# Attention with decaying state and a two-expert adapter: loads in tile order, two-chunk frames, unread products at the start, shared copies and a new order

## The chip, the core and the metric

The kernel runs on one core of one Trainium2 chip. A core has five engines that run their own instruction streams and meet at semaphores: TensorE (PE, with its weight loads shown apart as PEld), VectorE (DVE), ScalarE (ACT), GpSimd (POOL) and SyncE (SP), which issues most transfers. Sixteen DMA engines move data between HBM and the on-chip memory SBUF; PE writes its products to PSUM, which has eight banks. The metric is device time in microseconds (us): 98.98 is the median of three runs (98.64 to 99.32).

## What is computed

Four sequences with eight heads, 768 tokens and 48 channels pass a linear attention whose state decays by w per token and channel; the outputs of the heads, side by side (384 channels), get the weighted sum of the two best of eight rank-16 adapters:

```python
for t in range(S):                                   # per batch and head
    cur = einsum('bhd,bhe->bhde', u[None] * kt, vt)
    y[:, :, t] = einsum('bhd,bhde->bhe', rt, state + cur)
    state = wt[..., None] * state + einsum('bhd,bhe->bhde', kt, vt)
...
logits = x @ w_gate                                  # x: y as (3072, 384)
topk = the 2 largest of 8; w = softmax over these 2
out = x + sum over the 2 experts e of w[e] * (x @ A[e]) @ B[e]
```

## The kernel before

The work is cut into 24 tiles of 128 tokens: four sequences of six tiles. Heads are handled in four pairs; a pair stands on 128 partitions as two heads of 48 channels, each padded to 64 with zeros. One tile passes these steps (functions of the same names; lines as in the profile):

- **Loads.** load_rk brings r and k of a tile (512 KB) into a ring of ten (RING), load_w brings w of two tiles (384 KB; tiles 0 and 1 alone), both issued by SP. load_v is issued by POOL and turns v into bf16 on the way: one, two and three chunks at the start, then six at a time, into four buffers. consts.0, consts.1 and consts.2 load u, the matrix A with the gate, and B; castc (L164, POOL) turns them into bf16.
- **Decay.** ln (L176, ACT) takes log w; cs (L186, PE) sums it along the tile with four products with a triangle of ones, into x_ps, a single bank; expp (L191, ACT) and expm (L196, ACT) make the exponentials of plus and minus that sum.
- **Products with the decay.** rmul (L205, POOL) makes rd from r and expp, kmul (L210, DVE) makes kd_ from k and expm, qmul (L200, POOL) makes q = r k.
- **The own token.** dgmm (L228, PE) multiplies q with u per pair, four products of eight columns; dv (L241, DVE) scales v with the result; ymd (L280, PE) adds it to y_ps.
- **Inside the tile.** amm (L249, PE) multiplies kd_ with rd into a_ps, aev (L254, DVE) masks it into at, ymv (L295, PE) multiplies that with v into y_ps.
- **The state.** ktr (L223, PE) transposes kd_, ktev (L235, ACT) copies it to ks, kv (L264, PE) adds ks times v to the state s_ps, resc (L270, DVE) scales the state with the tile's whole decay, and sev (L275, ACT) copies it to sb; ymS (L289, PE) multiplies the previous tile's sb with rd into y_ps. The last tile of a sequence does none of the state's steps but ymS.
- **The output of attention.** yev (L300, ACT) copies y_ps to xT.
- **The gate**, for three tiles at once (the last three tiles as two and one): zl (L314, PE) makes logits and x A; top (L326 and L328, DVE) finds the largest and the differences, gexp (L334, ACT), gsel (L340, DVE), gmul (L347, POOL), gnorm (L353 and L354, DVE) and gmul2 (L360, POOL) make the weights g, zw (L366, DVE) scales x A, zT (L375, PE) transposes it, zTev (L381, DVE) copies it.
- **The result.** dmm (L389 and L391, PE) adds x and the adapters' share in PSUM, oev (L396, ACT) copies to res, store (L400, SP) writes it.

PSUM is full: a_ps takes two banks, x_ps, kd, y_ps and s_ps one each, and z_ps, zT_ps and d_ps share two.

The order of each engine's instructions is written out by hand in ORDER, a list of "step.tile"; an engine takes its own steps from it strictly in that order, and semaphores see to what it needs from others. A step whose engine waits holds everything behind it on that engine. The list was made by a planner from costs of the steps.

## Time and profile before

| | |
|---|---|
| median of three runs | 98.98 us |
| the profiled execution | 97.83 us, its span 96.1 us |
| busy: PE, DVE, ACT, POOL | 73.8, 75.6, 72.9, 67.0 us |
| mean granted clock of PE | 0.987 |
| DMA | 25.09 MB, mean 261 GB/s |

The span runs from the first to the last instruction of one profiled execution; the rest of its 97.83 us lies around it. A row of a group gives busy time, mean duration of one, and the idle time of its engine just before, with what ended it. Durations of neighbours on an engine overlap a little, so that sums of durations are longer than the busy time.

### The profile page before, as it was taken

To read this page: it belongs to the slowest core of one execution; us is meant where nothing else is said; L and a number is where in the kernel's file an instruction comes from. 1 tells how busy PE (TensorE), PEld (TensorE's weight loads), DVE (VectorE), ACT (ScalarE), POOL (GpSimd) and SP (SyncE) were. 2 spreads that over 40 slices of the span, in tenths; PEclk is the share of its full clock that TensorE was granted. 3 is DMA by queue.
4 is the path that set the end of the run, shared out by engine and by line. 5 is a ranking of instruction groups with operands and counts; after the bars stand their busy time and mean duration, and the time that the engine had idled before them with its cause. 6 is when DMAs were issued, how large, how long until landed. Compare 5 with 4: busy or idle time off the path is not lost.

```text
span 96.1 us, 3361 instructions
## 1 busy us (share of the span) xinstructions
PE 73.8 (77%) x1312; PEld 56.5 (59%) x1312; DVE 75.6 (79%) x180; ACT 72.9 (76%) x159; POOL 67.0 (70%) x85
## 2 busy tenths in 40 slices
PE   0204069999989997999899889989998898987230
PEld 0103057787867775787778667867776695754010
DVE  5423427978599999999999999999999999984320
ACT  5347148785699789999999989999999996663410
POOL 7581089996099969999999589899918997200000
PEclk9999999999999999999999999999999999999995
DMA  2999999999999506999999999889618842215402
GB/s 56 318 243 285 317 412 422 413 419 312 275 412 380 201 24 162 388 322 215 375 422 406 403 409 229 237 291 405 238 51 240 328 159 96 83 67 186 163 1 82
DMA packets 10096, 25.09 MB, mean 261 GB/s; under 512 B 1248, under 2 KB 4960, under 8 KB 10080
## 3 DMA queue, kind: packets, MB, share of 16 engines
q1 hardware_dynamic: 9216, 22.52, 62.5%
q0 software_dynamic: 864, 2.36, 13.3%
q8 instruction: 10, 0.16, 0.7%
q14 instruction: 6, 0.05, 0.2%
HBM read 22.51 MB, written 4.72 MB: 283 GB/s over the span
## 4 chain that ended last, share of the span: by engine, by line
DVE 39%; PE 36%; issue 11%; POOL 4%; ACT 4%; DMA 3%; POOLq 0%; ACTq 0%; DVEq 0%
DVE at L254 11%; DVE dv L241 6%; PE z_ps L314 5%; PE y_ps L295 5%; PE kd L223 4%; PE x_ps L186 4%; PE a_ps L249 4%; DVE zw L366 3%; DVE s_ps L270 3%; PE y_ps L280 3%; PE y_ps L289 3%; DMA w_in<-in_w_dram 3%; PE d_ps L391 2%; DVE tp L326 2%; PE kd L228 2%
## 5 line engine op out<-in xcount | busy, mean ns | idle before, releaser
L254 DVE TENSOR_TENSOR at<-a_ps,mask 128x1024 bf16<-128x1024 f32 x24 | 29.1, 1213 | 3.6 <-PE a_ps L249 3.6
L200 POOL TENSOR_TENSOR q<-rk 128x512 bf16<-128x512 f32 x24 | 30.2, 1267 | 0.0
L205 POOL TENSOR_TENSOR rd<-rk,ep 128x512 bf16<-128x512 f32 x24 | 28.1, 1179 | 1.8 <-ACT ep L191 1.6
L191 ACT ACTIVATE ep<-x_ps 128x512 f32<-128x512 f32 x24 | 14.4, 602 | 5.1 <-PE x_ps L186 4.7
L186 PE MATMUL x_ps<-tri,lw 128*128 128x128 f16 x96 | 10.7, 242 | 8.1 <-ACT lw L176 6.9
L300 ACT CAST xT<-y_ps 128x512 bf16<-128x512 f32 x24 | 14.1, 590 | 2.7 <-PE y_ps L295 2.7
L396 ACT COPY res<-d_ps 128x384 f32<-128x384 f32 x24 | 11.3, 490 | 4.6 <-PE d_ps L391 4.1
L196 ACT ACTIVATE x_ps<-x_ps 128x512 f32<-128x512 f32 x24 | 14.4, 601 | 0.0
L241 DVE TENSOR_TENSOR dv<-v_bf,kd 128x384 bf16<-128x384 bf16 x24 | 13.0, 544 | 1.2 <-PE kd L228 1.1
L186 PEld LDWEIGHTS <-lw 128*128 128x128 f16 x96 | 6.7, 107 | 10.4 <-ACT lw L176 7.5
L176 ACT ACTIVATE lw<-w_in 128x768 f16<-128x768 f32 (+1 forms) x13 | 10.3, 793 | 2.7 <-DMA w_in<-in_w_dram 2.7
L347 POOL TENSOR_TENSOR pe<-sel,ge 128x24 f32<-128x24 f32 (+2 forms) x9 | 2.1, 228 | 13.9 <-ACT ge L334 9.5
L295 PE MATMUL y_ps<-at,v_bf 128*48 128x128 bf16 x192 | 10.4, 233 | 1.3 <-DVE at L254 1.1
L235 ACT COPY ks<-kd 128x384 bf16<-128x384 bf16 x20 | 9.6, 482 | 2.0 <-PE kd L223 1.5
L280 PE MATMUL y_ps<-ident,dv 128*128 128x128 bf16 x96 | 10.0, 231 | 0.1
L289 PE MATMUL y_ps<-rd,sb 48*48 48x128 bf16 x160 | 8.5, 229 | 0.7 <-ACT sb L275 0.7
L228 PE MATMUL kd<-ub,q 128*128 128x8 bf16 x96 | 6.1, 169 | 3.9 <-POOL ub L164 3.9
L295 PEld LDWEIGHTS <-v_bf 128*48 128x48 bf16 x192 | 6.7, 107 | 3.4 <-issue 1.6
L391 PE MATMUL d_ps<-b_b,zT 128*128 128x384 bf16 x24 | 7.8, 327 | 0.4 <-DVE zT L381 0.2
L389 PE MATMUL d_ps<-ident,xT 128*128 128x96 bf16 x96 | 8.1, 207 | 0.0
L314 PE MATMUL z_ps<-aw_b,xT 128*128 128x136 bf16 x96 | 7.8, 235 | 0.3 <-ACT res L396 0.3
L270 DVE TENSOR_TENSOR s_ps<-s_ps,ep 128x192 f32<-128x192 f32 x20 | 7.2, 359 | 0.9 <-PE s_ps L264 0.7
(151 smaller groups left out, 130.1 us busy)
## 6 DMA issues: line engine op xcount, KB each, us to landing
rk<-in_rk_dram SPq DMA_DIRECT2D x24, 512.0 KB, 8.2
out_dram<-res SPq DMA_DIRECT2D x24, 192.0 KB, 2.9
w_in<-in_w_dram SPq DMA_DIRECT2D x11, 384.0 KB, 8.3
v_bf<-in_v_dram POOLq DMA_DIRECT2D x3, 576.0 KB, 9.0
w_in<-in_w_dram SPq DMA_DIRECT2D x2, 192.0 KB, 3.9
v_bf<-in_v_dram POOLq DMA_DIRECT2D x1, 288.0 KB, 8.8
aw_f<-in_aw_dram SPq DMA_DIRECT2D x1, 272.0 KB, 10.2
v_bf<-in_v_dram POOLq DMA_DIRECT2D x1, 192.0 KB, 7.6
```

The lines of the kernel that those rows point to most:

```text
L186: nc.tensor.matmul(x_ps[:, p, :], lhsT=lwof(t, p), rhs=tri, start=True, stop=True)
L191: nc.scalar.activation(out=ep[:, :, 1:L + 1], in_=st[t]["x"], func=ACT.Exp)
L196: nc.scalar.activation(out=x, in_=x, func=ACT.Exp, scale=-1.0)
L200: nc.gpsimd.tensor_mul(q, st[t]["rk"][:, 0], st[t]["rk"][:, 1])
L205: nc.gpsimd.tensor_mul(rd, st[t]["rk"][:, 0], st[t]["ep"][:, :, 0:L])
L241: nc.vector.tensor_mul(o[:, :, 0:D], vseq[t], dg.to_broadcast([128, H, D]))
L254: nc.vector.tensor_mul(at.rearrange("s g p f -> s (g p) f"), st[t]["a_ps"].rearrange("s g p f -> s (g p) f"), mask.to_broadcast([128, H, L]))
L280: nc.tensor.matmul(y_ps[:, p, :], lhsT=st[t]["dv"][:, 2 * p:2 * p + 2, :].rearrange("p a b -> p (a b)"), rhs=ident, start=(p == 0), stop=F ...
L289: nc.tensor.matmul(st[t]["y_ps"][s_, p, :], lhsT=st[t - 1]["sb"][s_, p, :], rhs=st[t]["rd"][s_, p, :], start=False, stop=False, skip_group ...
L295: nc.tensor.matmul(st[t]["y_ps"][g * 64:g * 64 + D, p, :], lhsT=vseq[t][:, h, :], rhs=st[t]["at"][:, g, p, :], start=False, stop=(h >= H - ...
L300: nc.scalar.copy(out=xT, in_=st[t]["y_ps"])
L314: nc.tensor.matmul(z_ps[:, i, :], lhsT=st[t0 + i]["xT"][:, p, :], rhs=aw_b[:, p, :], start=(p == 0), stop=(p == P - 1))
```

## The change

- Rings: twelve rk tiles instead of ten, four buffers of log w instead of three, q three instead of two, rd six instead of three, kd_ five instead of two, res six instead of four. v comes in loads of three chunks into six buffers.
- Loads are listed strictly by tile on SP. The first is followed by rk.0, w.1, u, rk.1, w.2 and so on up to rk.14 ahead of the first store; rk.15 to rk.21 follow store.5.
- warm(n) issues n products of 512 columns of zeros into a bank that nobody reads: nine ahead of cs.0, seven behind it, five behind cs.1 and two behind cs.2.
- Filled pads: the sixteen pad rows of the first three pairs carry pieces of the fourth pair's r and k, so qmul works on three pairs instead of four and dgmm issues three products instead of four. The values are only placed by the host.
- Two-chunk frames: the running sum of the decay goes over two tiles. An odd tile's cs has four more products (with ones, over the tile before); expp writes into a frame of two tiles (four of them); resc is done behind odd tiles only.
- Shared copies: some ktev, sev, oev move to DVE, some zTev to ACT, rmul.1 and castc.2 to DVE.
- For the last gate (one tile) gsel and gmul become one DVE instruction, and gmul2 and zw another.
- ORDER is a new list.

The diff, cut:

```diff
+PQ = P - 1
-RING = 10
+RING = 12
+VL = 3
+VB = 6
+Q_ON_DVE = ()
+R_ON_DVE = (1,)
+CAST_ON_DVE = (2,)
+KT_ON_DVE = (0, 1, 2, 6, 12)
+S_ON_DVE = (1, 6, 8, 16)
+Y_ON_DVE = ()
+OUT_ON_DVE = (10, 15, 22)
+ZT_ON_ACT = (2, 17, 20)
 ORDER = """
...
+warm.9 load_v.0 load_v.1 load_w.0 load_rk.0 ln.0 cs.0 warm.7 load_w.1 expp.0 ln.1 expm.0 rmul.0 kmul.0 amm.0
+aev.0 cs.1 warm.5 expp.1 expm.1 consts.0 castc.0 load_rk.1 qmul.1 rmul.1 load_w.2 load_rk.2 ln.2 load_rk.3
+load_w.4 load_rk.4 qmul.0 dgmm.0 load_v.3 kmul.1 amm.1 cs.2 warm.2 aev.1 expp.2 expm.2 rmul.2 dv.0 ktr.0
+ymd.0 ktev.0 ymv.0 kv.0 yev.0 sev.0 qmul.2 kmul.2 dgmm.1 dv.1 amm.2 aev.2 cs.3 expp.3 expm.3 rmul.3 ktr.1
+ktev.1 ymd.1 ymS.1 ymv.1 kmul.3 dgmm.2 dv.2 kv.1 resc.1 sev.1 ln.4 cs.4 ktr.2 ktev.2 yev.1 ymd.2 ymS.2
+qmul.3 dgmm.3 dv.3 expp.4 expm.4 kmul.4 kv.2 load_v.6 sev.2 amm.3 aev.3 ktr.3 ktev.3 ymv.2 yev.2 cs.5 expp.5
...
+aev.10 gexp.8 gmul.8 gnorm.8 gmul2.8 cs.12 expp.12 expm.12 rmul.12 dmm.5 oev.5 store.5 load_v.15 kv.10
+sev.10 dgmm.11 dv.11 qmul.14 qmul.13 kmul.12 ymd.10 ymS.10 ymv.10 yev.10 zw.8 amm.11 aev.11 dgmm.12 dv.12
+cs.13 expp.13 expm.13 rmul.13 zT.8 zTev.8 ln.14 ymd.11 ymS.11 ymv.11 yev.11 load_rk.15 qmul.15 load_w.16
+load_rk.16 load_rk.17 load_w.18 load_rk.18 load_rk.19 load_w.20 load_rk.20 load_rk.21 amm.12 ktr.12 dmm.7
+oev.7 store.7 kmul.13 cs.14 expp.14 expm.14 rmul.14 dmm.6 oev.6 store.6 ktev.12 dgmm.13 aev.12 dv.13 zl.11
...
+aev.23 dmm.18 oev.18 store.18 zl.22 kv.22 sev.22 top.22 gexp.22 gsel.22 gmul.22 gnorm.22 dmm.20 oev.20
+store.20 ymd.23 ymS.23 ymv.23 yev.23 gmul2.22 zw.22 zT.22 zTev.22 dmm.21 dmm.22 oev.21 oev.22 store.21
+store.22 zl.23 top.23 gexp.23 gmul.23 gnorm.23 zw.23 zT.23 zTev.23 dmm.23 oev.23 store.23
 """
+    zero = const.tile([128, 512], BF16)
+    nc.vector.memset(zero, 0.0)
+    ones = const.tile([128, 128], FP16)
+    nc.vector.memset(ones, 1.0)
-    NLW = 3
+    NLW = 4
-    NEP = 3
+    NEP = 4
-        t_ = const.tile([128, P, L + 1], F32, name=f"ep{i}")
+        t_ = const.tile([128, P, WL * L + 1], F32, name=f"ep{i}")
+    def warm(n):
+        if not idle:
+            idle["ps"] = pp.tile([128, 512], F32, name="idle_ps", tag="m", bufs=2)
+        for _ in range(n):
+            nc.tensor.matmul(idle["ps"], lhsT=zero[:, 0:128], rhs=zero, start=True, stop=True)
+    def copy(on_dve, o, i):
+        if on_dve:
+            nc.vector.tensor_copy(out=o, in_=i)
+        else:
+            nc.scalar.copy(out=o, in_=i)
-        n = {0: 1, 1: 2, 3: 3}[t] if t < NC else NC
-        v_bf = wk.tile([128, NC, H, D], BF16, name="v_bf", bufs=4)
+        n = {0: 1, 1: 2, 3: 3}[t] if t < NC else VL
+        v_bf = wk.tile([128, VL, H, D], BF16, name="v_bf", bufs=VB)
-            nc.tensor.matmul(x_ps[:, p, :], lhsT=lwof(t, p), rhs=tri, start=True, stop=True)
+            nc.tensor.matmul(x_ps[:, p, :], lhsT=lwof(t, p), rhs=tri, start=True, stop=t % WL == 0)
+            if t % WL:
+                nc.tensor.matmul(x_ps[:, p, :], lhsT=lwof(t - 1, p), rhs=ones, start=False, stop=True)
-        nc.gpsimd.tensor_mul(q, st[t]["rk"][:, 0], st[t]["rk"][:, 1])
+        (nc.vector if t in Q_ON_DVE else nc.gpsimd).tensor_mul(q, st[t]["rk"][:, 0, 0:PQ], st[t]["rk"][:, 1, 0:PQ])
-        for p in range(P):
+        for p in range(PQ):
...
-        if t % NC < NC - 1:
+        if t % WL == WL - 1 and t % NC < NC - 1:
             d_ = st[t]["ep"][:, :, L:L + 1]
             nc.vector.tensor_mul(s_ps, s_ps, d_.to_broadcast([128, P, D]))
...
+        if n == 1:
+            nc.vector.scalar_tensor_tensor(out=pe[:, 0], in0=st[t]["z_ps"][:, 0, ER:ER + E], scalar=st[t]["tp"][:, 0, 1:2],
+                                           in1=st[t]["ge"][:, 0], op0=ALU.is_ge, op1=ALU.mult)
...
+    for j in range(2 * PQ):
+        c = j % 3 * 16
+        rk[:, :, j % 2, D:64, :, j // 2] = rk[:, :, j // 3, c:c + 16, :, PQ]
```

## The prediction

> **What bounds the kernel now.** I read the page's slices first, then a table of busy time by stage, then the chain of waits, the groups of instructions and the DMA views.

> ```profile
> span 96.1 us, 3361 instructions
> PE   0204069999989997999899889989998898987230
> DVE  5423427978599999999999999999999999984320
> DMA  2999999999999506999999999889618842215402
> ```

> The slices are 2.4 us each. VectorE (DVE) is full from slice 12 to slice 35, and has holes ahead of that and behind it. The stages, cut at instructions that I name below (columns: busy time of PE, PEld, DVE, ACT, POOL with counts, granted clock, DMA share, GB/s):

> ```profile
> 7.55:12.57 5.02, 1.15 (x12) 0.79 (x13) 1.91 (x2) 1.84 (x3) 0.27 (x3) 1.00 1.11 312
> 12.57:16.40 3.83, 3.63 (x49) 2.76 (x49) 2.06 (x4) 2.82 (x6) 3.83 (x4) 1.00 1.03 416
> 16.40:20.40 4.00, 4.00 (x55) 3.36 (x56) 3.64 (x5) 3.07 (x7) 3.98 (x5) 1.00 1.03 416
> 20.40:24.40 4.00, 4.00 (x55) 3.17 (x53) 2.87 (x5) 2.90 (x7) 2.74 (x3) 1.00 1.06 341
> 29.08:79.66 50.58, 47.12 (x923) 36.78 (x919) 49.78 (x117) 48.34 (x109) 45.02 (x49) 1.00 0.81 277
> 84.28:96.10 11.82, 4.74 (x68) 3.03 (x66) 4.21 (x17) 3.66 (x10) 0.84 (x4) 0.89 0.27 101
> ```

> Three regimes. The middle (29.08 to 79.66, seventeen tiles, 2.98 us each) belongs to DVE: 49.78 of 50.58 us, with ACT (48.34) and PE (47.12) close behind. The start holds a hole (7.55 to 12.57, in which every compute engine is idle for more than half the time while the DMA engines are full) and then a stretch in which PE is full and DVE isn't. The end is a chain of single instructions. The start in detail, from the order of time, where a bracket gives the idle time before and its releaser, and from the chain (the lines with two numbers, a name and a count):

> ```profile
> 6.97 0.52 ACT L176 ACTIVATE lw<-w_in 128x384 f16<-128x384 f32 x1 [1.40 <-DMA w_in<-in_w_dram]
> 11.08 0.69 DVE L210 TENSOR_TENSOR kd__180<-rk,x_ps 128x512 bf16<-128x512 f32 x1 [1.04 <-DMA rk<-in_rk_dram]
> 12.31 0.21 POOL L164 CAST ub<-ub_f 128x32 bf16<-128x32 f32 x1 [4.75 <-DMA ub_f<-in_ublk_dram]
> 14.42 0.69 DVE L210 TENSOR_TENSOR kd__217<-rk,x_ps 128x512 bf16<-128x512 f32 x1 [1.01 <-ACT x_ps L196]
> 28.99 0.68 DVE L210 TENSOR_TENSOR kd__537<-rk,x_ps 128x512 bf16<-128x512 f32 x1
> 14.05 0.43 PE y_ps L280 x4
> 23.86 1.37 PE z_ps L314 x12
> 29.08 0.59 DVE kd__537 L210
> 39.77 0.22 PE y_ps L280 x4
> ```

> The hole is the wait for the small u load (POOL until 12.31) and for tile 1's rk (DVE until 11.08). The three kmul lines with brackets or shapes are tiles 1, 2 and 6; the chain has tile 6's again with 0.59, its time without the 0.09 in which it overlaps the instruction before. The two L280 lines are the same four products of 128 columns: 0.43 us early, 0.22 later, while the granted clock reads 1.00 in both stages. So PE ran at half its later rate from 12.57 until about the z products at 23.86, although it was busy for 11.63 of those 11.83 us.

> [...]

> **The change part by part: the start.** Durations, by groups (busy us, mean ns):

> ```profile
> L254 DVE TENSOR_TENSOR at<-a_ps,mask 128x1024 bf16<-128x1024 f32 x24 | 29.1, 1213 | 3.6 <-PE a_ps L249 3.6
> L241 DVE TENSOR_TENSOR dv<-v_bf,kd 128x384 bf16<-128x384 bf16 x24 | 13.0, 544 | 1.2 <-PE kd L228 1.1
> L270 DVE TENSOR_TENSOR s_ps<-s_ps,ep 128x192 f32<-128x192 f32 x20 | 7.2, 359 | 0.9 <-PE s_ps L264 0.7
> L381 DVE COPY zT<-zT_ps 128x384 bf16<-128x384 bf16 x7 | 2.4, 349 | 0.0
> L326 DVE MAX8 tp<-z_ps 128x8 f32<-128x8 f32 x24 | 2.6, 161 | 2.9 <-PE z_ps L314 2.5
> L366 DVE TENSOR_TENSOR zw<-z_ps,g 128x384 bf16<-128x384 f32 x7 | 3.9, 550 | 0.1
> L164 POOL CAST b_b<-b_f 128x384 bf16<-128x384 f32 x1 | 0.5, 499 | 0.0
> L200 POOL TENSOR_TENSOR q<-rk 128x512 bf16<-128x512 f32 x24 | 30.2, 1267 | 0.0
> L235 ACT COPY ks<-kd 128x384 bf16<-128x384 bf16 x20 | 9.6, 482 | 2.0 <-PE kd L223 1.5 <-ACT xT L300 0.2
> L396 ACT COPY res<-d_ps 128x384 f32<-128x384 f32 x24 | 11.3, 490 | 4.6 <-PE d_ps L391 4.1
> L191 ACT ACTIVATE ep<-x_ps 128x512 f32<-128x512 f32 x24 | 14.4, 602 | 5.1 <-PE x_ps L186 4.7
> rk<-in_rk_dram SPq DMA_DIRECT2D x24, 512.0 KB, 8.2
> v_bf<-in_v_dram POOLq DMA_DIRECT2D x1, 288.0 KB, 8.8
> q0 software_dynamic: 432, 0.59, 31.5%
> ```

> The last line is the v queue in the first 12 us: 31.5% of 12 us, 3.8 us of all DMA engines, for six chunks of v. The change leaves three of them for later (1.9 us freed), and puts w.2 (384 KB) behind rk.1 and u ahead of both. At 312 GB/s w.2 is 1.2 us. So rk.1 should land some 3 us earlier than 11.08, near 8, and u earlier than that. The hole shrinks, and what bounds the start instead is a chain that the warm-up makes longer: nine unread products of 512 columns at 0.43 us, from about 1.2 us, hold PE until 5.0, so cs.0 ends at 5.6. ACT now takes ln.1 ahead of expm.0, and w.1 lands at 6.97: ln.1 ends at 7.5, expm.0 (taken as L191) at 8.1, kmul.0 (0.69) at 8.8, amm.0 (two times 0.3) at 9.4, aev.0 (1.21) at 10.6. Then, all on DVE: rmul.1 (moved from POOL; priced as kmul, 0.69, the other end L200's 1.27) to 11.3, kmul.1 to 12.0, 0.6 for amm.1, aev.1 to 13.8, dv.0 (0.54) to 14.4, ktev.0 to 14.7. kmul.2 starts at 14.7, against 14.42 before, but with aev.1, rmul.1 and ktev.0 done. The small cast moves only within POOL, and qmul.1 ahead of qmul.0 is covered by rmul.1's and amm.1's times.

> From kmul.2 to kmul.6 the new order gives DVE three more kmul besides kmul.2 (0.59 each), four dv (0.46), three aev (1.14), resc.1 and resc.3 and sev.1 (0.28 each), two ktev (0.30), the gate of tiles 0 to 2 (three tp, four small ones taken as tp, zw: 7 x 0.16 + 0.55, and less the overlap 1.6) and the cast of B (0.45, by its 0.50 on POOL). Each is its group's mean less some 0.08 of overlap. That is 2.36 + 1.84 + 3.42 + 0.84 + 0.60 + 1.6 + 0.45 = 11.1 us. kmul.6 would start at 25.8 if DVE never waited. One wait shows: load_v.3 is behind qmul.0 on POOL, so it is issued near 11.3 and lands at 20.1 (8.8), and dv.3 is due at 19.3. I put 0.6 us down for it and its like: kmul.6 at 26.4 instead of 28.99, **-2.6 us**; without any wait -3.2. This needs PE at full rate. Nothing before 12.57 is as dense as the warm-up, and the flip came at the z products, the first long run of wide full-height products; so I take it as warm. The cover gone (PE cold until 24 us), the gain is about 0: the stretch is PE's as before, with three odd tiles' extra products (3 x 0.43 = 1.3) against its start 1.1 us earlier.

> **The middle.** From kmul.6 on, resc falls from sixteen to six; tile 22's lies beside the gate's chain and counts nothing: 9 x 0.359 = -3.2. Shared copies: ktev 6 and 12 on DVE by the zT copy of the same size, 2 x 0.349 (ACT's 482 ns the other end) = +0.7; sev 6, 8, 16 by L270, 3 x 0.359 = +1.1; oev 10, 15, 22 by dv, 3 x 0.544 (ACT's 490 the other end) = +1.6; zTev 2, 17, 20 away, -1.05. Sum **-0.8**. ACT loses two 482, three 490 and three sev and gets two zT back, POOL loses a quarter of q (24 x 0.32 = 7.6 by size; 0 if q has a fixed price). Neither sets the pace, so neither counts. POOL pays three more v issues. The wider rings for q, rd, kd_, res and lw, the two-frame ep and the memsets (before the first load lands) cost nothing on the path.

> PE pays: each odd tile issues four more products of 128 columns, 0.22 to 0.38 us, nine tiles, +2.0 to +3.4; the fourth product of dgmm goes (the filled pads carry it), 17 x 0.05 = -0.8.

> ```profile
> 38.65 0.38 PE x_ps L186 x4
> 38.27 0.19 PE kd L228 x4
> rk<-in_rk_dram SPq DMA_DIRECT2D x1, 512.0 KB, 4.2
> ```

> Net +1.2 to +2.6 against the 3.46 us in which PE idles in the middle. The new order's waits can't be read off a profile of the old one. Ends: -0.8 (DVE's 0.80 idle goes) and +2.6 (PE sets the pace and keeps its idle time). I take **+0.8**, nearer to the cover than to its loss, since DVE waited only 0.80 us under the old order.

> **The end.** The last gate, one tile:

> ```profile
> 90.50 0.20 POOL L347 TENSOR_TENSOR pe<-sel,ge 128x8 f32<-128x8 f32 x1 [3.32 <-ACT ge L334]
> 90.93 0.16 DVE L354 RECIPROCAL den<-den 128x1 f32<-128x1 f32 x1
> 91.24 0.20 POOL L360 TENSOR_TENSOR g<-pe,den 128x8 f32<-128x8 f32 x1 [0.54 <-DVE den L354]
> 91.47 0.29 DVE L366 TENSOR_TENSOR zw<-z_ps,g 128x128 bf16<-128x128 f32 x1 [0.38 <-POOL g L360]
> ```

> gmul2's step goes: zw follows den at once, 91.12 instead of 91.47. gmul on DVE saves about 0.05. oev.22 on DVE stands beside oev.21, and zl.23 still waits for oev.21. **-0.4.**

> **Sum.** -2.6 - 0.8 + 0.8 - 0.4 = -3.0. The profiled execution took 97.83 us (span 96.1), so 94.8 by its own; it lies 1.15 below the median of the runs, 98.98, to which I apply the sum: 96.0.

> **The rivals.**

> PE stays cold (B). For it: 11.63 busy of 11.83 us did not warm it before. Against: the warm-up is denser. The start gains nothing: 98.98 - 0.8 + 0.8 - 0.4 = 98.6. The unread products would then be without effect on the rate.

> PE becomes the pace of the middle (C): +2.6 instead of +0.8, 97.8. For it: 47.12 of 50.58 busy already. Against: busy counts pipelined ends, and 3.46 us are free.

> Late loads of tiles 15 to 21 (D), the slower side. On SP they now stand behind store.5, which waits for oev.5, behind expm.12. From the end T of expp.12, oev.5 ends at T + 1.1 (0.60 + 0.49), and rk.15 lands at T + 1.1 + L. POOL reaches qmul.15 behind rmul.13, which follows expp.13 (T + 3.0, one tile on), so by T + 4.3 (1.27, as L200), and rmul.14, due at T + 6, stands behind qmul.15 (0.95): late by L + 1.1 + 0.95 - 6 = L - 3.95. With L = 4.2, seen once in a quiet stretch, that is 0.3 and hidden; with the median 8.2 it is 4.25, and the time is 96.0 + 4.25 = 100.2. It turns slower than before by 1% at L = 7.9. Against it, by then the first fifteen tiles are in, and the queue is empty.

> **How the numbers follow.** About 1% is what a measurement of this kernel can tell from no change: 97.99 to 99.97. Forecast 0.57 (96.0; its own range 92.8 to 97.9: all terms at their good ends, -3.2 - 0.8 - 0.8 - 0.4 = -5.2, give 93.8, less one for the 1.15 between profile and median), C 0.11 (97.8, still faster), B 0.15 (98.6, same), D 0.17 (100.2, slower). Faster 0.68, same 0.15, slower 0.17. The range, 92.8 to 99.0, takes in B and leaves out D and a little at the low end.

> **What would show it.** Right: L280's groups take 0.22 before 15 us; POOL's wait for u ends before 9; kmul.6 starts near 26.4; DVE stays over 97% busy from there to aev.23; the last den to zw gap is under 0.05. Wrong: 0.43 at 20 us (B); PE at 98% with DVE waiting for PE in the middle (C); POOL waiting for a DMA near tile 15 (D); or dv waiting for v, which I priced for tile 3 alone.

## The result and the profile after

The changed kernel takes 94.99 us (median of six runs, 94.59 to 96.03), the kernel before 98.81 in the runs beside it: a ratio of 0.968, interval 0.960 to 0.977. The forecast was 96.0. Ratios here and below compare only those executions of each kernel that lie within some 1.5% of its fastest, medians take in all of them, so the two need not agree.

The profiled execution of the changed kernel happens to be the longest of its six (96.03 us, span 94.3), while that of the kernel before lies below its median. A second profile of the very same kernel, taken for the first experiment, has a span of 91.6. The two differ above all in the granted clock, so both are shown: the one below is "after", the other "again".

The page's slices of after:

```profile
span 94.3 us, 3426 instructions
DVE  5803965978999999999999999989999998974620
PEclk9999995559999999999999999999999999999955
```

And of again:

```profile
span 91.6 us, 3426 instructions
DVE  5907778989999999999999999999989998973710
PEclk9999999999999999999999999999999999999855
```

The granted clock of after is at half (0.50) in slices 7 to 9 (14.0 to 20.8 us); again keeps it until the last slices. The order of time in after, at the places that the prediction named:

```profile
7.78 0.20 POOL L197 CAST ub<-ub_f 128x24 bf16<-128x24 f32 x1 [0.24 <-DMA ub_f<-in_ublk_dram]
9.83 2.40 POOL L236 TENSOR_TENSOR q<-rk 128x384 bf16<-128x384 f32 x2 [1.84 <-DMA rk<-in_rk_dram]
15.01 0.63 PE L316 MATMUL y_ps<-ident,dv 128*128 128x128 bf16 x4
15.53 0.68 DVE L246 TENSOR_TENSOR kd__275<-rk,x_ps 128x512 bf16<-128x512 f32 x1
18.25 0.63 PE L316 MATMUL y_ps<-ident,dv 128*128 128x128 bf16 x4
28.46 0.67 DVE L246 TENSOR_TENSOR kd__614<-rk,x_ps 128x512 bf16<-128x512 f32 x1
89.26 0.16 DVE L397 RECIPROCAL den<-den 128x1 f32<-128x1 f32 x1
89.45 0.35 DVE L412 SCALAR_TENSOR_TENSOR zw<-z_ps,den,pe 128x128 bf16<-128x128 f32 x1
```

The wait for u is gone (12.31 before), tile 1's rk lands at 9.8, and ymd's four products (L316, L280 before) still take 0.63 us from first start to last end, as in this view of the kernel before at half rate (16.73 us; 0.38 at 27.53, at full rate). In again the same four, and tile 6's kmul:

```profile
13.82 0.39 PE L316 MATMUL y_ps<-ident,dv 128*128 128x128 bf16 x4
26.00 0.68 DVE L246 TENSOR_TENSOR kd__614<-rk,x_ps 128x512 bf16<-128x512 f32 x1
```

With PE at full rate tile 6's kmul starts at 26.00, without it at 28.46, against 28.99 before. The table of stages for the stretch from that kmul to the last aev (columns as in the prediction), before, after and again:

```profile
28.99:84.28 55.29, 51.47 (x1007) 39.90 (x1004) 54.03 (x126) 51.41 (x116) 47.04 (x52) 1.00 0.76 262
```

```profile
28.46:82.60 54.14, 52.21 (x1012) 41.27 (x1010) 52.96 (x121) 50.22 (x112) 43.39 (x53) 1.00 0.80 266
```

```profile
26.00:79.92 53.92, 52.26 (x1012) 41.20 (x1010) 52.92 (x122) 50.08 (x112) 43.26 (x53) 1.00 0.83 284
```

DVE works 1.1 us less and waits 1.2 and 1.0 us instead of 1.3; PE works 0.8 us more. Behind it, from the last aev's start to the span's end, lie 11.82 us before, 11.70 after and 11.68 in again. So against the profile before, start, middle and end change by -0.5, -1.2 and -0.1 us in after, and by -3.0, -1.4 and -0.1 in again.

### The profile page after: what moved, and what is told of

Same layout as the page of the kernel before. It is cut to its first block, busy times and chain, and to the rows that moved or that the text cites. A ratio compares the mean times of both kernels' runs of the same rounds, so it can differ in the third digit from the quotient of the medians.

```text
span 94.3 us, 3426 instructions
## 1 busy us (share of the span) xinstructions
PE 80.9 (86%) x1359; PEld 59.7 (63%) x1359; DVE 77.6 (82%) x183; ACT 69.9 (74%) x150; POOL 61.2 (65%) x84
## 3 DMA queue, kind: packets, MB, share of 16 engines
q0 software_dynamic: 1296, 2.36, 14.1%
## 4 chain that ended last, share of the span: by engine, by line
DMA 42%; DVE 23%; PE 9%; SPq 8%; issue 7%; ACT 4%; POOL 3%; POOLq 0%; ACTq 0%
DMA rk<-in_rk_dram 35%; DVE at L290 9%; DMA w_in<-in_w_dram 7%; SPq L180 4%; SPq L174 4%; DVE dv L277 3%; DVE zw L419 2%; ACT res L163 1%; PE d_ps L444 1%; PE z_ps L350 1%; DVE den L396 1%; POOL q L236 1%; POOL pe L390 1%; PE d_ps L442 1%; PE zT_ps L428 1%
## 5 line engine op out<-in xcount | busy, mean ns | idle before, releaser
L241 POOL TENSOR_TENSOR rd<-rk,ep 128x512 bf16<-128x512 f32 x23 | 27.2, 1183 | 9.1 <-ACT ep L227 9.0
L236 POOL TENSOR_TENSOR q<-rk 128x384 bf16<-128x384 f32 x24 | 24.3, 1020 | 2.4 <-DMA rk<-in_rk_dram 2.2
L163 ACT COPY res<-d_ps 128x384 f32<-128x384 f32 x21 | 10.2, 484 | 5.2 <-PE d_ps L444 4.5
L219 PE MATMUL x_ps<-tri,lw 128*128 128x128 f16 x96 | 12.1, 230 | 0.8 <-DVE kd__1701 L246 0.3
L316 PE MATMUL y_ps<-ident,dv 128*128 128x128 bf16 x96 | 9.8, 227 | 0.1
L219 PEld LDWEIGHTS <-lw 128*128 128x128 f16 x96 | 8.1, 102 | 2.6 <-issue 1.2
L157 PE MATMUL idle_ps<-zero 128*128 128x512 bf16 x23 | 8.4, 523 | 1.2 <-DVE zero L102 1.2
L163 ACT COPY ks<-kd 128x384 bf16<-128x384 bf16 x15 | 7.3, 487 | 0.9 <-PE kd L259 0.5
L350 PE MATMUL z_ps<-aw_b,xT 128*128 128x136 bf16 x96 | 7.2, 223 | 0.2 <-ACT res L163 0.2
L316 PEld LDWEIGHTS <-dv 128*128 128x128 bf16 x96 | 6.8, 102 | 0.5 <-issue 0.2
L221 PE MATMUL x_ps<-ones,lw 128*128 128x128 f16 x48 | 7.0, 227 | 0.0
## 6 DMA issues: line engine op xcount, KB each, us to landing
rk<-in_rk_dram SPq DMA_DIRECT2D x24, 512.0 KB, 10.2
v_bf<-in_v_dram POOLq DMA_DIRECT2D x7, 288.0 KB, 7.0
```

The costliest lines, as they stand in the source:

```text
L163: nc.scalar.copy(out=o, in_=i)
L219: nc.tensor.matmul(x_ps[:, p, :], lhsT=lwof(t, p), rhs=tri, start=True, stop=t % WL == 0)
L236: (nc.vector if t in Q_ON_DVE else nc.gpsimd).tensor_mul(q, st[t]["rk"][:, 0, 0:PQ], st[t]["rk"][:, 1, 0:PQ])
L241: (nc.vector if t in R_ON_DVE else nc.gpsimd).tensor_mul(rd, st[t]["rk"][:, 0], st[t]["ep"][:, :, 0:L])
L316: nc.tensor.matmul(y_ps[:, p, :], lhsT=st[t]["dv"][:, 2 * p:2 * p + 2, :].rearrange("p a b -> p (a b)"), rhs=ident, start=(p == 0), stop=F ...
```

## The experiments: what the start is made of

**Again, more unread products, none, and qmul.0 first.** Four kernels on one chip, 98.31 us for the kernel before there. The first is the changed kernel with no edit.

> The changed kernel once more, beside the others on one chip. Theory (call it rate): the profiled execution shows a granted clock of 0.50 from 14 to 20 us, and executions differ in how long that lasts (0.935 to 0.978 mean clock); so a second look should give 94.6 to 95.6 us, and a span that is shorter where the mean clock is higher. Rival (chain): the start is set by loads and by the order on POOL, the clock doesn't matter; then span and mean clock go without relation.

Measured: 95.17 us (93.35 to 95.90), ratio 0.976 (0.961 to 0.991). Over the twelve executions of both sets, the five with a mean clock of 0.935 to 0.938 have spans of 93.3 to 94.3 (mean 93.8), the seven with 0.961 to 0.978 have 91.6 to 93.7 (mean 92.8). So a lower clock goes with a span longer by about one us; it doesn't explain all of the scatter. The kernel before scatters more (95.86 to 101.45 over its 18 executions here).

```diff
-warm.9 load_v.0 load_v.1 load_w.0 load_rk.0 ln.0 cs.0 warm.7 load_w.1
+load_v.0 load_v.1 load_w.0 load_rk.0 ln.0 cs.0 load_w.1
...
-cs.1 warm.5
+cs.1
...
-cs.2 warm.2
+cs.2
```

> The changed kernel without the 23 unread products. Rate theory: PE stays at half rate until the z products, as before the change; the start loses what the warm-up gives, 1 to 2 us, so 96 to 97 us, and tile 6's kmul comes at 29 to 30 us. Chain rival: the unread products only delay cs.0 (5.0 instead of 3.8 us), so without them 94 to 95 us, no slower than the changed kernel.

Measured: 97.93 us, ratio 1.007 (0.999 to 1.015): by the ratio nothing of the change's gain is left. Tile 6's kmul comes at 28.12, and the profile has a second loss, which the rate has no part in. Its middle is 55.29 us long, as long as before the change, because of this (POOL, then DVE):

```profile
52.72 1.00 POOL L236 TENSOR_TENSOR q<-rk 128x384 bf16<-128x384 f32 x1 [2.07 <-DMA rk<-in_rk_dram]
55.08 0.18 DVE L396 TENSOR_REDUCE den<-pe 128x3 f32<-128x24 f32 x1 [1.52 <-POOL pe L390]
```

That is qmul.15: POOL waits for rk.15, which SP issued at 46.38, behind store.5; the gate's step behind it on POOL comes late, and DVE stands. It is the prediction's rival D, at a landing time of at most 6.3 us and a price of 1.2 (55.29 against 54.14).

```diff
-cs.0 warm.7
+cs.0 warm.9
...
-cs.1 warm.5
+cs.1 warm.11
...
-cs.2 warm.2
+cs.2 warm.7
```

> The changed kernel with 36 unread products instead of 23 (9, 9, 11 and 7), which fill PE's idle time ahead of amm.0, dgmm.0 and ktr.0. Rate theory: the granted clock no longer falls to 0.50, dv and ktev no longer wait for PE, tile 6's kmul comes near 27 us instead of 28.5, and the time falls by 1 to 1.5 us to about 93.7. Chain rival: no change within 0.5 us.

Measured: 94.69 us (93.91 to 94.92), ratio 0.985 (0.976 to 0.994). In its profile the granted clock stays at 1.00 through the start (4 to 28 us) and tile 6's kmul comes at 26.52, span 92.3. So the fall was kept off here, and all six executions lie within 1.0 us, where again's spread over 2.5. The median isn't lower by the 1 to 1.5 us expected: only some executions of the changed kernel have the fall, and where there is none, tile 6's kmul comes half a us later than in again (26.52 against 26.00).

```diff
-castc.0 load_rk.1 qmul.1
+castc.0 qmul.0 load_rk.1 qmul.1
...
-load_rk.4 qmul.0 dgmm.0
+load_rk.4 dgmm.0
```

> The changed kernel with qmul.0 ahead of qmul.1 on POOL, so that it no longer stands behind the wait for tile 1's rk (landed at 9.8 us); dgmm.0 could run near 10 instead of 12.3. Chain rival: the start moves up by up to 1.5 us, 93.5 us. Rate theory: amm.1 still waits for kmul.1 (12.0 us), so no more than 0.4 us, but the gap on PE is shorter, and with it the fall of the clock perhaps later.

Measured: 96.17 us, ratio 0.986 (0.968 to 1.005). dgmm.0 ran at 10.39 instead of 12.29, and amm.1 came no earlier (12.99, 12.45 in after). It waits for kmul.1, which stands behind rmul.1 on DVE; in this profile rk.1 landed at 10.80, one us later than in after, and rmul.1 took 1.51 us instead of 0.83, with a qmul on POOL beside it. So an earlier dgmm.0 gains nothing while amm.1 waits for rk.1; the later landing keeps this run from showing more.

**The unread products alone, on the kernel before.** Another chip, 97.00 us before.

```diff
+    zero = const.tile([128, 512], BF16)
+    nc.vector.memset(zero, 0.0)
...
-cs.0
+warm.7 cs.0 warm.7
...
-dgmm.0
+warm.18 dgmm.0
```

> The kernel before, with unread products alone: seven ahead of cs.0, seven behind it and eighteen ahead of dgmm.0, where PE waits for the u load until 12.6 us. Rate theory: PE is at full rate when the work of tiles 1 to 4 begins, four products take 0.22 us there, tile 6's kmul comes at 26.5 to 27 instead of 29.0 us, 96 to 97 us in all. Rival: the start is bound by loads and by the order, 98 to 99 us.

Measured: 95.58 us (94.94 to 96.10), ratio 0.998 (0.989 to 1.007). The ratio shows no difference and the medians differ by 1.4 us, so the gain in time isn't settled by these runs. The profile is plain:

```profile
14.57 0.39 PE L293 MATMUL y_ps<-ident,dv 128*128 128x128 bf16 x4
26.92 0.68 DVE L223 TENSOR_TENSOR kd__572<-rk,x_ps 128x512 bf16<-128x512 f32 x1
```

ymd is at full rate, tile 6's kmul comes at 26.92 instead of 28.99, -2.07 us, and the middle is what it was (55.30 against 55.29). Of the start's -3.0 us in again, about two thirds would be the unread products, the rest loads and order, if the kernel before always reached full rate as late as in its profile. It needn't: the kernel with the frames alone, further down, has no unread products and the old start, and ymd's four products run there at full rate by 16.96 us:

```profile
16.96 0.39 PE L285 MATMUL y_ps<-ident,dv 128*128 128x128 bf16 x4
```

The same step took 0.63 us before the change (16.73). With the full rate, tile 6's kmul came there at 27.02, as early as with the unread products. That can be why the ratio shows no difference here; no run shows it.

## The experiments: what the middle is made of

Five kernels undo one part of the change. Four keep the new list (the one without frames gets the added resc in it); the third puts the old list back and keeps the parts. The first three ran with the one just shown (97.00 us before), two with those further down (98.13 before).

```diff
-KT_ON_DVE = (0, 1, 2, 6, 12)
-S_ON_DVE = (1, 6, 8, 16)
-OUT_ON_DVE = (10, 15, 22)
-ZT_ON_ACT = (2, 17, 20)
+(all four empty)
```

> The changed kernel with all of ktev, sev and oev on ACT and all of zTev on DVE. My prediction's sum (DVE alone is the pace): DVE loses two ktev, three sev and three oev (3.4 us) and gets two or three zTev (1.05 us) between tile 6's kmul and the end, so the kernel gets faster by some 2.4 us, to 92.6. Rival (ACT is level with DVE): ACT gets 2.7 us back and becomes the pace; no gain, up to 2 us slower.

Measured: 109.68 us (107.56 to 110.72). Both expectations missed by far. No engine got too much work: in the middle, 60.99 us long here, ACT is busy for 50.11 us and DVE for 52.34. It is waits, up to 2.13 us at one place in the middle. The start grows too (tile 6's kmul at 33.15), and the longest wait lies there, 4.64 us at tile 3. The links of that ring, from the orders of time of ACT, PE and DVE:

```profile
19.05 0.32 ACT L163 CAST sb<-s_ps 128x192 bf16<-128x192 f32 x1 [1.17 <-DVE s_ps L306]
19.26 0.85 ACT L209 ACTIVATE lw<-w_in 128x768 f16<-128x768 f32 x1
20.16 0.61 PE L219 MATMUL x_ps<-tri,lw 128*128 128x128 f16 x4 [1.81 <-ACT lw L209]
21.29 0.48 ACT L163 COPY ks<-kd 128x384 bf16<-128x384 bf16 x1 [1.18 <-PE kd L259]
21.66 0.59 ACT L163 CAST xT<-y_ps 128x512 bf16<-128x512 f32 x1
22.30 0.58 PE L316 MATMUL y_ps<-ident,dv 128*128 128x128 bf16 x4 [1.11 <-ACT xT L163]
23.65 0.55 DVE L277 TENSOR_TENSOR dv<-v_bf,kd 128x384 bf16<-128x384 bf16 x1 [4.64 <-PE kd L264]
```

sev.1, now on ACT, waits there for DVE's resc.1. ln.4 stands behind it, cs.4 on PE behind ln.4, ktr.2 behind cs.4; ktev.2 on ACT waits for that, yev.1 stands behind ktev.2, ymd.2 waits for yev.1's bank, and dgmm.3, for which dv.3 waits, stands behind ymd.2. The list had put a copy there that DVE could do at once after resc.1.

```diff
-            if t % WL:
-                nc.tensor.matmul(x_ps[:, p, :], lhsT=lwof(t - 1, p), rhs=ones, start=False, stop=True)
...
-        if t % WL == WL - 1 and t % NC < NC - 1:
+        if t % NC < NC - 1:
```

> The changed kernel with frames of one tile again: no extra products with ones, resc behind every tile but a sequence's last (12 more on DVE), eight one-tile buffers of the exponentials; resc.t put right behind kv.t in the order. Theory (DVE is the pace): nine of the twelve lie between tile 6's kmul and the last aev, so that stretch grows from 54.0 us by 9 x 0.28 to 0.36, to 56.5 to 57.2 us, and the time by about 3 us to 98. Rival (PE is the pace there): PE loses 36 products in that stretch, 2 to 3 us, and the stretch stays within 0.7 us of 54.

Measured: 104.55 us, ratio 1.093 (1.084 to 1.102). The middle grew to 60.37 us, by 6.2, of which DVE's own work is 2.6 (55.51 busy): the theory's size is in it, with 3.7 us of added waits, in part beside a granted clock of 0.94 on average in that stretch. The start is longer as well (tile 6's kmul at 30.92).

```diff
-VL = 3
-VB = 6
+VL = 6
+VB = 4
...
+(ORDER of the kernel before)
```

> All parts of the change but the order: the old order list (no unread products in it, v in six-chunk loads into four buffers as that list needs), with two-chunk frames, filled pads, larger rings, shared copies and the fused last gate. Theory (DVE is the pace; start limited by the half rate and by the late u load): start as before the change, tile 6's kmul at 28.5 to 29.5 us, then the stretch to the last aev 0.5 to 1.5 us shorter than the old 55.3: 97 to 98 us. Rival (the copies are shared for the new list, and do harm under the old one): 99 us or more.

Measured: 106.41 us, ratio 1.110 (1.101 to 1.119). The stretch is 65.20 us, with DVE busy for 54.54 of it, in the longest of its four executions (109.02). The parts under the old list are far slower than the old kernel under the same list.

```diff
-PQ = P - 1
+PQ = P
...
-        rk[:, :, j % 2, D:64, :, j // 2] = rk[:, :, j // 3, c:c + 16, :, PQ]
```

> The changed kernel without the filled pads: q over four pairs again, four products in dgmm. My prediction: POOL has slack, PE pays 0.05 us per tile; no change within 0.5 us, the stretch from tile 6's kmul to the last aev stays at 54 us. Rival (the list fits its own costs only, so that any part undone under it costs several us): q 0.25 us longer per tile delays rmul and with it amm, 1 us or more slower.

Measured: 97.27 us, ratio 1.012 (1.005 to 1.019); the middle:

```profile
28.17:83.56 55.39, 52.90 (x1030) 41.92 (x1028) 53.24 (x122) 50.31 (x112) 47.92 (x53) 1.00 0.78 261
```

55.39 against 54.14, with POOL at 47.92 instead of 43.39. POOL is still idle for 7.5 us, and yet the stretch is 1.3 us longer: DVE's reduction waits for POOL's gate step (1.2 us in three places, 0.5 in two in after), which stands behind the longer q on POOL. Its start has the clock's fall too (0.50 from 16 to 20 us), with tile 6's kmul at 28.17.

```diff
-OUT_ON_DVE = (10, 15, 22)
+OUT_ON_DVE = ()
```

> The changed kernel with oev.10, oev.15 and oev.22 back on ACT, the three largest of the shared copies. My prediction's sum (DVE is the pace, ACT has slack): 2 x 0.46 less in the stretch from tile 6's kmul to the last aev, 53 us, and about 1 us faster. Rival (ACT is level with DVE and the list fits its own costs): ACT's expp and yev come later by 0.5 us at tiles 10 and 15, the stretch grows by 0.5 us or more.

Measured: 95.35 us, ratio 0.992 (0.987 to 0.997); the middle:

```profile
26.70:80.83 54.13, 52.23 (x1012) 41.26 (x1010) 52.43 (x119) 50.64 (x114) 43.27 (x53) 1.00 0.82 277
```

DVE works 0.5 us less than in after, and the stretch is as long as there (54.13 against 54.14): the time became idle time. Neither expectation is met.

**The frames alone, on the kernel before.** The frames' part of the change, with its buffers, and nothing else:

```diff
+            if t % WL:
+                nc.tensor.matmul(x_ps[:, p, :], lhsT=lwof(t - 1, p), rhs=ones, start=False, stop=True)
...
-        ep = eps[t % NEP]
+        ep = eps[t // WL % NEP]
+        o = t % WL * L
...
-        if t % NC < NC - 1:
+        if t % WL == WL - 1 and t % NC < NC - 1:
```

> The kernel before with the two-chunk frames alone (12 resc fewer on DVE, 48 products more on PE, four two-tile buffers of the exponentials, four of log w), under the old list. DVE-pace theory: the stretch from tile 6's kmul to the last aev falls from 55.3 by 9 x 0.28 to 52.8 us, the time by 2 to 3 us. Rival (the list fits its own costs only): the extra products delay expp under the old list, and the stretch stays above 55.

Measured: 98.35 us, ratio 1.011 (1.003 to 1.020); the middle:

```profile
27.02:83.37 56.35, 52.68 (x1042) 41.56 (x1040) 52.48 (x117) 51.01 (x116) 47.05 (x52) 1.00 0.81 272
```

DVE works 1.55 us less than before (52.48 against 54.03), and the stretch is 1.06 us longer. PE works 1.2 us more. So the frames' relief for DVE is real, and under the old list all of it is lost in waits.

**A better version?** The 36 unread products, and the loads of tile 15 on earlier.

```diff
-store.2 ymd.7
+store.2 load_rk.15 load_w.16 load_rk.16 load_rk.17 ymd.7
...
-load_rk.15 qmul.15 load_w.16 load_rk.16 load_rk.17 load_w.18
+qmul.15 load_w.18
```

> An attempt at a better version: 36 unread products (as in the kernel with more of them), and rk.15, w.16, rk.16 and rk.17 issued behind store.2 instead of behind store.5. Theory: the clock does not fall, POOL's waits for rk near tile 15 go: span 91 to 92 us in the profile, 0.5 to 1 us less than the changed kernel in the median. Rival: stores wait behind these loads and hold res; no gain.

Measured: 94.26 us (93.97 to 95.49), ratio 0.980 (0.975 to 0.985). The granted clock stays (1.00 from 10.6 to 14.0 us and in the middle), POOL's only wait for an rk is the one for tile 1 (1.6 us), and the middle is 53.66 us, the shortest of all. In time it can't be told from the changed kernel (0.968 and 0.976 in its two sets).

## Why the prediction was right, point by point

**The start, -2.6 us: the term holds where its condition holds.** kmul.6 was forecast at 26.4 and came at 26.00 in again; it came at 28.46 in after. The prediction priced the full rate as given or not given (rival B) for the whole start; it is given and then lost. The traces list the stretches of the granted clock with start and length, and they show when. In after the rate rises at 7.18 us, falls at 14.01, rises at 20.84 and holds for 68.27 us; in again it rises at 4.55 and holds for 81.92; before the change it rises at 25.27 and holds for 68.27. The stretches between two changes (6.83, 6.83, 68.27 and 81.92 us) are whole multiples of 3.41. One of about 3.41 itself shows with the oev back on ACT: the clock reads 0.74 on average from 12 to 16 us and 0.83 from 16 to 20, which makes 3.4 us at 0.50. So PE's work is read here in steps of 3.41 us, counted from the first rise, which came at 7.18 and 4.55 us in two executions of one kernel: first in after, then in again (columns as in the prediction):

```profile
7.18:10.60 3.42, 2.50 (x25) 1.26 (x23) 1.88 (x3) 1.66 (x4) 1.33 (x3) 1.00 1.04 361
10.60:14.01 3.41, 1.65 (x19) 0.80 (x18) 2.50 (x4) 1.92 (x4) 2.28 (x4) 1.00 1.03 417
14.01:17.42 3.41, 2.79 (x40) 2.33 (x40) 2.38 (x6) 1.10 (x3) 2.03 (x2) 0.50 1.06 355
17.42:20.84 3.42, 3.42 (x46) 2.79 (x45) 2.59 (x5) 2.43 (x4) 2.09 (x3) 0.50 1.05 377
```

```profile
4.55:7.97 3.42, 2.44 (x21) 1.13 (x19) 0.70 (x2) 1.61 (x3) 1.32 (x2) 1.00 1.07 270
7.97:11.38 3.41, 1.84 (x20) 0.98 (x16) 2.77 (x3) 1.93 (x3) 2.58 (x3) 1.00 1.03 404
11.38:14.79 3.41, 2.39 (x44) 1.67 (x42) 2.45 (x4) 1.29 (x3) 2.28 (x3) 1.00 1.03 411
```

In after PE's gaps ahead of 14 us fall largely into one step, in which PE is busy for 1.65 of 3.41 us, and the rate is at half behind it, to the end of a step that PE fills (3.42 of 3.42). In again the steps lie elsewhere against the same program, the gaps are shared between two of them (1.84 and 2.39 us busy), and the rate holds. In the last kernel above, the attempt at a better version, they lie where they do in after (its rate rises at 7.19), and it has 13 more unread products:

```profile
10.60:14.01 3.41, 2.86 (x25) 1.39 (x24) 2.50 (x4) 1.71 (x3) 2.28 (x4) 1.00 1.02 413
```

Its rate holds. So among these three starts the fall goes with the least busy step (1.65 us, against 1.84 and 2.86 without a fall). That this, and with it the place of the steps, is the reason why only some executions have the fall is the author's estimate from these three; it isn't shown for the others. The prediction's own reason for the full rate, that the flip came at the z products, doesn't hold: without the unread products ymd's four products take 0.63 us at 17.89 and 0.39 at 20.83, and with the frames alone 0.39 at 16.96, while the first reader of the z products, tp on DVE, starts at 24.75 and 23.28. That dense work by itself brings the full rate isn't shown either: before the change PE was busy without a gap from 15.03 us on, and the rate rose at 25.27.

In its profile the kernel without the unread products has tile 6's kmul at 28.12 against 26.00 in again; the rest of its loss there is the middle, with the late load of rk.15.

What the prediction had as steps of the chain was near: cs.0 forecast to end at 5.6 (5.63 in after), kmul.0 to start at 8.1 (8.15), kmul.2 at 14.7 (15.53); in again, with the rate earlier, 5.18, 6.92 and 14.30. rk.1 landed at 9.8, not near 8, and it cost nothing in after, as aev.0 ended at 10.6 and rmul.1 could not start earlier. dv.3 did not wait for v.

**The middle's work, -0.8:** near, measured -1.1 (54.03 to 52.96 busy). The sum counted oev.22 here, which stands behind the last aev; without it the terms give -1.4, by means that count the overlaps of neighbours twice.

**The middle's new waits, +0.8:** mis-sized, measured -0.1 to -0.3 (idle 1.26 before, 1.18 and 1.00). The new list leaves no more waits on DVE than the old, with PE at 96% of the stretch (52.21 of 54.14) where rival C had it set the pace. PE's added work was priced at 1.2 to 2.6 us and measured 0.7 to 0.8 (51.47 to 52.21 and 52.26).

**"Neither sets the pace, so neither counts" (ACT's and POOL's relief): this step was wrong.** Undoing the filled pads, which by this step cost nothing, lengthened the middle by 1.3 us with POOL idle for 7.5. Taking two oev off DVE, which by the same step should have shortened it by their whole time, changed nothing. With DVE at 98, PE at 96 and ACT at 93% under one fixed list, no single engine's work sets the pace alone; the order of the list counts with it, through waits that go around from engine to engine. Such a ring is shown above for one place of the start; for the middle it is argued from these two kernels, with one profile each. The sum did not show the error: the middle came out 1.2 to 1.4 us shorter where its two terms cancel to nothing, and which part of the change brought that isn't shown.

**The end, -0.4: right in the gate, lost behind it.** den to zw went from 0.54 to 0.19 us from start to start, as worked out. But the step before it came no earlier against the last aev (den starts 6.65 us behind it before, 6.66 in after), PE is at half rate in the last slices (0.50 from 89.10 us), and the last product (0.35 before) takes 0.51.

**The sum.** -3.0 forecast; -3.8 by the medians, 3.2% (2.3 to 4.1) by the ratio. That it came so near is in part luck: the start gave -0.5 or -3.0 by execution, the middle -1.2 to -1.4 instead of 0.0, the end -0.1 instead of -0.4.

**Rival D** was there and small: 0.39 us of waiting on POOL for the later rk in after, 2.07 without the unread products; the landing of rk.15 took at most 4.2 us in after (issued at 46.71, qmul.15 at 50.94 without a wait) and 6.3 without the unread products, under the 7.9 from which it decides.

What stays open: what decides on the rate (PE's busy time in a step alone doesn't, by the counts below); how much of the start's gain the kernel before has by itself in executions that reach full rate early; and what the frames and the shared copies are worth with a list of their own, which wasn't tried. The kernels that undo them show only that the list and the parts belong together.

## What to carry to other kernels

When three engines are within a few per cent of each other under a fixed order, don't price an edit by its engine's busy time alone: look for what stands behind the moved instruction on its new engine, and follow it around until it comes back. A part undone under a list that was planned with it measures the list's fit, not the part's worth; read its own work from the busy times of the stretch instead. And look at an execution's granted clock before comparing two profiles: here two executions of one kernel differed by 2.7 us (94.3 and 91.6), more than the whole start was forecast to gain.
